# Attention block, exponentials on two engines: line 2 of most early chains added in place by a transfer, and another planned duration for VectorE's score passes

## The chip, the cores and the metric

The kernel runs on one core of a Trainium2 chip. A core has TensorE (PE; its weight loads are shown as PEld), VectorE (DVE), ScalarE (ACT), GpSimd (POOL) and SyncE (SP), each with its own in-order queue of instructions, and 16 DMA engines. The metric is the device time of one execution in microseconds, the median of several executions.

## What is computed

A multi-head attention block with its projections, for one sequence of 2048 rows, 448 columns, 16 heads of 28:

```python
B, S, D, H = 1, 2048, 448, 16
...
Dh = D // H
qkv = (lambda x, *d: x.transpose(*d))((x @ wqkv).reshape(B, S, 3, H, Dh), 2, 0, 3, 1, 4)
q, k, v = qkv[0], qkv[1], qkv[2]
scores = jnp.einsum("bhqd,bhkd->bhqk", q, k) * (Dh ** -0.5)
p = _softmax(scores, axis=-1)
o = jnp.einsum("bhqk,bhkd->bhqd", p, v)
return (lambda x, *d: x.transpose(*d))(o, 0, 2, 1, 3).reshape(B, S, D) @ wo
```

Inputs and output are bf16.

## The kernel before, in words

**Tiling.** The 16 heads form four groups `g` of four heads, each head padded to 32 partitions. The 2048 queries form four chunks `c` of 512. A pair (g, c) is a set; there are 16 sets, in the order of `ORDER`. A set has 64 score blocks: four heads times 16 blocks of 128 keys. A block is a product of 128 keys by 512 queries (line 780), made with the queries' tile `QP` and the keys' tile `KA`. Blocks of different heads use different rows of the array, and two or three run at once.

**Two engines make the exponentials.** ScalarE takes two blocks at a time from a PSUM tile `a` (two banks used in turn) and writes exponentials `pt` (line 978; ten buffers). VectorE takes single blocks from the banks `d0`, `d1` or `m` (line 993): it adds a bias and clamps at zero, as int16, and the bits read as bf16 are a piecewise linear approximation of 2 to the score's power. Four such blocks of one set, one for each head, form a chain in one tile `I` (128 x 2048, named `I4`). For a better approximation the chain is used three times: as it is (line 0), with 43 added to the bits (line 1, tile `J1`) and with 85 added (line 2, tile `J2`), each multiplied by V scaled with its own weight (`WT`; line 616 makes the scaled copies). So each VectorE block costs three products with V instead of one. All products of a set are accumulated in the bank `o` (line 1123); a column of ones in V gives the softmax's denominator.

**How lines 1 and 2 are made.** In the plain way VectorE adds the constant in one pass over the chain (line 1064). A chain that begins while at least `FAR` = 30 blocks of its set are left, in any set but the first and the last, is far: GpSimd fills `J1` with 43 (line 1029) and issues a transfer that adds `I` to it (line 1040, 512 KB), and VectorE makes line 2 only. There are four buffers of `I` and `J1`, three of `J2`.

**GpSimd** also squares K and Q for their norms (line 357) and multiplies each set's outcome by its reciprocal denominators (line 1173). `after_shared` places GpSimd's passes behind the VectorE pass that last used the port both share (`cur["shared"]`).

**What sets the order.** The kernel writes its whole instruction order by hand through a planner. `plan` simulates the engines with fixed durations (`D_EXP` 0.904 for an exponential pass, 0.6 for a score pass in `do_a`, `ACC_LAND` 5.6 from a transfer's issue to its landing, and so on), takes at each step what is ready, and emits it. Work other than the sets (projections, norms, V, output projection) stands in lists with needs, gates and priorities. `dve_ok` decides whether a block goes to VectorE: only if VectorE would be done with it before ScalarE is done with what it has. `pv_cands` sorts the products with V that are ready. Where TensorE would be idle for long, `dense` puts products with zeros. The plan is made with 24 seeds, and the one that the planner finds shortest is emitted. The engines then follow this order, held back by semaphores alone.

**V.** `VT[0]` holds V by group and block of 512 keys, groups 2 and 3 together; `VT[1]` and `VT[2]` hold the two scaled copies for all groups at once.

Of the kernel before, what the change touches and what calls it, by code (L numbers as in the profile page):

```python
# [53 lines left out]
def kernel(  # L54
# [7 lines left out]
    nc = tc.nc  # L62
# [28 lines left out]
    NPT = 10  # L91
    NCH = 4
    NCH2 = 3
    NJ = 4
    FAR = 30
    FIRST = 1
    RECLAG = 4.0
# [37 lines left out]
    WO = big.tile([P, G, D], BF16, name="WO")  # L135
    VT = [None] * NTERM
    for k in range(NTERM):
        VT[k] = {}
        for b in range(NXB):
            for g in range(GH):  # L140
                VT[k][g, b] = big.tile([P, XB, P], BF16, name=f"V{k}_{g}_{b}")[:]
        for b in range(NXB):
            t = big.tile([P, XB, G - GH, P], BF16, name=f"V{k}_{GH}_{b}")
            for g in range(GH, G):
                VT[k][g, b] = t[:, :, g - GH, :]
            VT[k][None, b] = t[:]
    xs = [big.tile([P, XB * D if b < NPL else (G - 1) * QW], BF16, name=f"xs{b}") for b in range(NXB)]
# [90 lines left out]
    def clear_v(g, b):  # L238
        v = VT[0][g, b]
        v = v.rearrange("p t g e -> p (t g e)") if g is None else v.rearrange("p t e -> p (t e)")  # L240
# [3 lines left out]
    for g in list(range(GH)) + [None]:  # L244
        for b in range(NXB):
            clear_v(g, b)
    for c in range(1, NQC):
        offs_rows(c, 0, nc.gpsimd)
    for c in range(NQC):
        offs_rows(c, 1, nc.gpsimd)  # L250

    nc.gpsimd.tensor_copy(out=identf[:], in_=ident[:])
    nc.gpsimd.memset(self_[:], 0.0)
# [4 lines left out]
    def plan(nc, tc, psum, big, wk, dram, seed, dry):  # L258
# [262 lines left out]
        def qn_first(bank, pri):  # L521
            def mm():
                held["qn0"] = (bank_tile(bank) if bank[0] != "a" else pair_tile(bank))[:, 0:QW]
                nc.tensor.matmul(out=held["qn0"], lhsT=maskK[:, 0, :], rhs=sqt.pop(("Q", 0, 0))[:], start=True, stop=True)

            def root():
                held["nq"] = VT[1][None, 0].rearrange("p t g e -> p (t g e)").bitcast(F32)
                nc.vector.tensor_scalar(out=held["nq"].bitcast(I32), in0=held.pop("qn0").bitcast(I32), scalar1=0.5,
                                        scalar2=float(127 << 22), op0=ALU.mult, op1=ALU.add)

            def scaled():
                su = held["su0"] = wk.tile([P, QW], BF16, name="su", bufs=1)
# [45 lines left out]
        def v_job(g, b, t0, bank, pri, gate=0, eng="DVE"):  # L578
# [7 lines left out]
            def mm(part):  # L586
                if part == 0:
                    held[key] = bank_tile(bank)
                for u in range(part * n // parts, (part + 1) * n // parts):
                    for cc in range(CC):  # L590
                        quarters(held[key][:, u * w:(u + 1) * w], xt(b, cc)[:, (t0 + u) * P:(t0 + u + 1) * P],
                                 WRAW[2][:, cc, g0 * HG * Dh:g1 * HG * Dh], cc == 0, cc == CC - 1)

            def evac():
                src = held.pop(key)[:, 0:n * w].rearrange("p (r e) -> p r e", e=Dh)
                if g is None:
                    dst = VT[0][None, b][:, t0:t0 + n, :, :].rearrange("p t g (i e) -> p (t g i) e", e=HP)
                else:
                    dst = VT[0][g, b].rearrange("p t (i e) -> p (t i) e", e=HP)
                if eng == "ACT":  # L600
                    nc.scalar.copy(out=dst[:, :, 0:Dh], in_=src)
                else:
                    nc.vector.tensor_copy(out=dst[:, :, 0:Dh], in_=src)

# [7 lines left out]

        def vs_job(g, b, pri):
            def scale(k):
                flat = (lambda v: v.rearrange("p t g e -> p (t g e)")) if g is None else (lambda v: v.rearrange("p t e -> p (t e)"))
                cur["shared"] = nc.vector.tensor_scalar(out=flat(VT[k][g, b]), in0=flat(VT[0][g, b]), scalar1=WT[k], scalar2=None, op0=ALU.mult)

            gs = [g] if g is not None else list(range(GH, G))
            for k in range(1, NTERM):
                add("DVE", 0.335 if g is None else 0.2, lambda k=k: scale(k), need=[("V", gs[0], XB * b + u) for u in range(XB)],  # L620
                    gives=[("VS", gg, b, k) for gg in gs], pri=pri + 0.1 * k, port=True)

# [110 lines left out]
        for b in range(NXB):  # L733
            v_job(1, b, 0, "m", 50 + b, STEPS + 10 + 12 * b)
            vs_job(1, b, 60 + b)
        a, z = 2 * STEPS, 2 * NQC * STEPS - 30
        for kt in range(0, NKT, 2):
            v_job(None, kt // XB, kt % XB, "m", 150 + kt, a + (z - a) * kt // NKT)
        for b in range(NXB):
            vs_job(None, b, 170 + b)  # L740
        for c in range(CL):
# [8 lines left out]
        pts_used = [0]  # L750
        chain = {"cur": None, "all": []}
        a_fifo = []
# [69 lines left out]
        def dve_ok(t, k):  # L822
            if chain["cur"] is None and len(chain["all"]) >= NCH:
                old = chain["all"][-NCH]
                if not j1_free() or not used_up(old, 0) or any(a[0] is old for a in adds) or old["acc"] is None or old["acc"] > t:
                    return False
            if chain["cur"] is not None and half_left(chain["cur"]["s"], 0) != half_left(chain["cur"]["s"], 1):
                return True
            fin = max(free["DVE"], t + 0.5) + 0.62 * (len(a_fifo) + k + 1) + 1.4 + 0.6 * sum(NTERM - a[2] for a in adds)
            return fin <= free["ACT"] + D_EXP * (len(exps) + max(0, left() // 2 - 2)) + 0.2 + shake(0.4)  # L830
# [29 lines left out]
        def d_more(s, t, acting):  # L860
            got, taken = [], []
            for b in d_banks(t):
# [8 lines left out]
                if ch is None:  # L871
# [3 lines left out]
                    ch[1] = wk.tile([P, HG * QW], I16, name="J1", bufs=NJ)  # L875
                    if sum(len(q) for q in remain[step[0]]) >= (FAR if step[0] < NSET - 1 else LASTFAR) and step[0] >= FIRST:
                        ch["far"] = True
# [112 lines left out]
        def do_a(t):  # L990
            r, b, pd, step, ch, n = a_fifo.pop(0)
            dst = ch["I"][:, n * QW:(n + 1) * QW]
            nc.vector.tensor_scalar(out=dst, in0=pd[:], scalar1=BIAS, scalar2=0.0, op0=ALU.add, op1=ALU.max)  # L993
            end = t + 0.6
            res[b] = end + LATS[("DVE", "PE")]
# [9 lines left out]
        def close(ch, m):  # L1005
            ch["m"] = m
            ch["at"] = free["DVE"]
            adds.append([ch, m, 2 if ch["far"] else 1])
            if ch["far"]:
                accumulate(ch, m)  # L1010

        def used_up(ch, k):
# [5 lines left out]
        def add_ok(a):  # L1018
            if a[2] == 1:
                return True  # L1020
            n = chain["all"].index(a[0])
            return n < NCH2 or used_up(chain["all"][n - NCH2], 2)

        def far_chain(ch):
# [8 lines left out]
            add("POOL", 1.05, emit, gives=[("fill", n)], pri=20, port=True)  # L1033

        def accumulate(ch, m):
            w = slice(0, m * QW)
# [5 lines left out]
            def landed(end):  # L1042
                at = ch["acc"] = end + ACC_LAND
                for n in range(m):
# [13 lines left out]
        def do_add(t):  # L1058
# [10 lines left out]
            adds[0][2] += 1  # L1069
            if adds[0][2] == NTERM:  # L1070
                adds.pop(0)
# [8 lines left out]
        def pv_cands(t):  # L1080
# [6 lines left out]
            for e in pending:  # L1087
                if e["step"][0] == s and e["ready"] <= t:
                    v = v_time(e)
                    if v is not None and v <= t:  # L1090
                        out_.append(e)
            out_.sort(key=lambda e: bool(e["ch"] and e["ch"]["far"] and e["k"] == 1 and t < e["ready"] + 1.5))
            return out_
# [14 lines left out]
        def do_pv(t, ws):  # L1108
# [9 lines left out]
            for w in ws:  # L1118
                for e in w:
                    _, i, j = e["step"]  # L1120
                    key = (s, i)
                    SETMM[key] = SETMM.get(key, 0) + 1
                    nc.tensor.matmul(out=o[HP * i:HP * (i + 1), :], lhsT=VT[e["k"]][g, j // XB][:, j % XB, HP * i:HP * (i + 1)],  # L1123
                                     rhs=e["ap"], start=(SETMM[key] == 1), stop=False, tile_position=(0, HP * i),
                                     skip_group_check=True)
                for e in w:
# [311 lines left out]
```

## Time and profile before

| What | us |
|---|---|
| Median of 3 runs (lowest to highest) | 360.37 (360.24 to 360.82) |
| The profiled execution | 360.86 |
| its span, first to last instruction | 359.1 |
| start of the first pass of line 978 | 16.9 |
| start of the last one | 349.0 |
| transfer of line 1040, issue to landing, least / median / most | 4.4 / 4.9 / 6.6 |

The clock that TensorE was granted is 0.998 over the span. The page's time by the profiler is the span; about 1.8 us of the execution lie around it. ScalarE's and TensorE's records overlap their neighbours (a pass of line 978 is recorded with 1.12 us and the next one starts 0.90 us after it), so the busy time of a group is the union of its records, and the pace is read from starts.

How the other work is spread: ten passes on ScalarE and 69 instructions on VectorE lie ahead of the first exponential pass (projections and norms of the first group, clearing of tiles); after the last one come the last set's normalisation, its output projection and the stores. In between all four engines work on the sets.

### The profile page before, as it was taken

What the parts mean: (1) busy time and instruction counts of PE and PEld (TensorE: products, weight loads), DVE (VectorE), ACT (ScalarE), POOL (GpSimd) and SP (SyncE); (2) the same over time, 40 slices, a digit from 0 to 9 for tenths busy, and PEclk for the clock granted to TensorE, in tenths of its full rate; (3) what the DMA queues carried; (4) which work ended last, traced back from release to release, by engine and by line L of the source; (5) the groups of instructions that cost most, each with busy time, mean ns of one, the idle gap of its engine ahead of it and who ended that gap; (6) DMA issues with size and microseconds to landing.
All of it is one profiled execution on the core that took longest, in us unless ns stands there. A gap on an engine that the chain in (4) does not pass through costs nothing.

```text
span 359.1 us, 11135 instructions
## 1 busy us (share of the span) xinstructions
PE 336.9 (94%) x4453; PEld 108.3 (30%) x4454; DVE 333.8 (93%) x615; ACT 339.1 (94%) x370; POOL 174.3 (49%) x215
## 2 busy tenths in 40 slices
PE   8999999999999999999989999998898989999995
PEld 4333233322234233232222222232222222222233
DVE  7889999999999999899999999998999999999973
ACT  3699999999999999999999999999999999999991
POOL 8951563635535474454455656464736464531010
PEclk9999999999999999999999999999999999999999
DMA  9430175664646666364667646565868848674111
GB/s 207 105 96 15 29 150 105 120 135 87 129 89 117 127 120 147 63 136 84 132 127 156 135 90 120 105 136 124 165 120 177 163 89 174 133 156 103 39 48 54
DMA packets 30185, 41.37 MB, mean 115 GB/s; under 512 B 15188, under 2 KB 21172, under 8 KB 30132
## 3 DMA queue, kind: packets, MB, share of 16 engines
q0 software_dynamic: 8368, 28.87, 41.6%
q1 hardware_dynamic: 20516, 11.22, 12.2%
q8 instruction: 35, 0.57, 0.6%
q10 hardware_dynamic: 1248, 0.55, 0.6%
q14 instruction: 18, 0.15, 0.1%
HBM read 6.20 MB, written 1.96 MB: 23 GB/s over the span
## 4 chain that ended last, share of the span: by engine, by line
PE 41%; ACT 32%; DVE 11%; issue 8%; DMA 6%; POOL 1%; SPq 0%; DVEq 0%; POOLq 0%; ACTq 0%
ACT pt L978 32%; PE a L780 14%; PE o L1123 11%; PE m L342 5%; DVE I L993 5%; PE m L335 4%; DMA J<-I 4%; DVE J L1064 2%; DMA rr<-scr 2%; PE o L679 1%; DMA scr<-rec 1%; PE d L780 1%; DVE KA L375 1%; DVE kp L451 1%; PE a L335 1%
## 5 line engine op out<-in xcount | busy, mean ns | idle before, releaser
L978 ACT ACTIVATE pt<-a 128x1024 bf16<-128x1024 f32 x358 | 330.5, 1121 | 3.5 <-PE a L780 1.6
L993 DVE TENSOR_SCALAR I<-d 128x512 int16<-128x512 f32 x276 | 180.3, 680 | 10.6 <-PE d L780 8.4
L780 PE MATMUL a<-QP,KA 32*128 32x512 bf16 (+1 forms) x708 | 138.1, 381 | 11.1 <-ACT pt L978 9.8
L1123 PE MATMUL o<-pt,V 128*32 128x512 bf16 x716 | 108.2, 383 | 0.0
L780 PE MATMUL d<-QP,KA 32*128 32x512 bf16 (+1 forms) x273 | 98.5, 383 | 0.2
L780 PEld LDWEIGHTS <-KA 32*128 32x128 bf16 (+1 forms) x1035 | 45.8, 91 | 145.0 <-issue 143.1
L1123 PE MATMUL o<-J,V 128*32 128x512 bf16 x616 | 87.2, 384 | 0.9 <-DVE J L1064 0.4
L1029 POOL MEMSET J<- 128x1024 int32 x55 | 58.4, 1061 | 48.4 <-PE d L780 13.5
L1040 POOL DMA_DIRECT2D J<-I x55 | 52.7, 957 | 58.1 <-DVE I L993 50.2
L1064 DVE TENSOR_SCALAR J<-I 128x2048 int16<-128x2048 int16 x99 | 73.9, 756 | 0.6
L1123 PE MATMUL o<-I,V 128*32 128x512 bf16 x308 | 68.2, 383 | 0.7 <-DVE o_sb L1150 0.6
L1123 PEld LDWEIGHTS <-V 128*32 128x32 bf16 x1640 | 31.3, 94 | 49.5 <-issue 45.3
L1173 POOL TENSOR_TENSOR xs<-o_sb,rr 128x512 bf16<-128x512 f32 x12 | 17.1, 1429 | 29.9 <-DVE J L1064 20.1
L357 POOL TENSOR_TENSOR sq<-QA 128x512 bf16<-128x512 bf16 x15 | 16.8, 1117 | 21.7 <-DVE QA L497 13.1
L993 DVE TENSOR_SCALAR I<-m 128x512 int16<-128x512 f32 x32 | 21.8, 680 | 0.2 <-PE m L780 0.2
L335 PE MATMUL m<-XT,WRAW 128*32 128x512 bf16 x216 | 18.3, 386 | 0.1
L357 POOL TENSOR_TENSOR sq<-KA 128x512 bf16<-128x512 bf16 x12 | 14.3, 1196 | 8.3 <-DVE KA L375 6.7
L342 PE MATMUL m<-WRAW,XT 128*32 128x112 bf16 (+1 forms) x432 | 13.7, 231 | 0.2
L342 PE MATMUL m<-WO,xs 128*32 128x448 bf16 x156 | 12.5, 359 | 0.0
L780 PE MATMUL m<-QP,KA 32*128 32x512 bf16 (+1 forms) x32 | 12.3, 384 | 0.0
L342 PE MATMUL m<-sq,maskK 128*32 128x512 bf16 x108 | 10.8, 389 | 1.4 <-POOL sq L357 1.2
L497 DVE CAST QA<-m 128x512 bf16<-128x512 f32 x15 | 10.2, 683 | 0.6 <-PE m L335 0.3
(126 smaller groups left out, 226.6 us busy)
## 6 DMA issues: line engine op xcount, KB each, us to landing
J<-I POOLq DMA_DIRECT2D x55, 512.0 KB, 4.9
rr<-scr SPq DMA_DIRECT2D x60, 64.0 KB
QP<-QA SPq DMA_DIRECT2D x60, 28.0 KB
out_dram<-osb SPq DMA_DIRECT2D x12, 112.0 KB
WRAW<-in_wqkv_dram SPq DMA_DIRECT2D x3, 336.0 KB
QP<-su SPq DMA_DIRECT2D x32, 2.0 KB
WO<-in_wo_dram SPq DMA_DIRECT2D x16, 24.5 KB
den<-o_sb SPq DMA_DIRECT2D x15, 8.0 KB
```

The lines of the kernel that those rows point to most:

```text
L335: nc.tensor.matmul(out=ps[HP * i:HP * (i + 1), :], lhsT=w[:, cc, h * Dh:h * Dh + HP], rhs=xt(c, cc), start=(cc == 0), stop=(cc == CC - 1), ...
L342: nc.tensor.matmul(out=out[r, :], lhsT=lhsT[:, r], rhs=rhs, start=start, stop=stop, tile_position=(0, HP * i), **k)
L357: after_shared(nc.gpsimd.tensor_tensor(out=t[:], in0=src, in1=src, op=ALU.mult))
L497: nc.vector.tensor_copy(out=t[:], in_=held[key][:, 0:QW])
L780: nc.tensor.matmul(out=out_ap, lhsT=KAt[(g, j // XB)][r, (j % XB) * P:(j % XB + 1) * P], rhs=q[r, :], start=(n == 0), stop=(n == len(terms ...
L978: nc.scalar.activation(out=pt[:], in_=ps[:], func=ACT.Exp, scale=LN2 / 128.0)
L993: nc.vector.tensor_scalar(out=dst, in0=pd[:], scalar1=BIAS, scalar2=0.0, op0=ALU.add, op1=ALU.max)
L1029: m = nc.gpsimd.memset(ch[1][:].bitcast(I32), fill)
L1040: after_shared(nc.gpsimd.dma_start(out=ch[1][:, w], in_=ch["I"][:, w], accum_op=ALU.add))
L1064: cur["shared"] = nc.vector.tensor_scalar(out=r[:, w], in0=ch["I"][:, w], scalar1=float(SHIFT[k]), scalar2=None, op0=ALU.add)
L1123: nc.tensor.matmul(out=o[HP * i:HP * (i + 1), :], lhsT=VT[e["k"]][g, j // XB][:, j % XB, HP * i:HP * (i + 1)], rhs=e["ap"], start=(SETMM[k ...
L1173: m = nc.gpsimd.tensor_tensor(out=otile(g, c), in0=st["o_sb"][:], in1=st["rr"][:], op=ALU.mult)
```

## The change

Chains come in three kinds. `own`: a chain that begins with at least `FAR2` = 44 blocks of its set left (in any set but the first and the last). VectorE makes its line 1 into `J1`. When that pass has read `I`, and TensorE has made the four products with `I` as it is, GpSimd issues a transfer that adds the constant tile `shift2` (85 in every element, filled once at the start) to `I` in place; `I` then is line 2. `far`: 30 to 43 blocks left, as before. All others: both lines by VectorE, as before.

So an own chain has no fill of `J1`, no tile `J2`, and its `I` is in use until line 2's products are done. There are six buffers of `I` and five of `J1`; room for them comes from V's scaled copies, which are now kept for two groups at a time (`VS` for groups 0 and 2, `VW` for groups 1 and 3), and made for group g once group g - 2 is finished. `VT` is one tile for group 1 and one for groups 2 and 3.

In the planner, a score pass lasts 0.615 instead of 0.6 (0.635 instead of 0.62 in `dve_ok`), a transfer's landing is counted behind the landing of the one before, at least `ACC_BUSY` = 3.0 after it (`landing`), and the products with the raw scores of an own chain go ahead of others. The last set's copy and one tile of the start (`nq`) use buffers of `pt` instead of V's.

```diff
@@ -89,10 +89,12 @@
...
     NPT = 10
-    NCH = 4
+    NCH = 6
     NCH2 = 3
-    NJ = 4
+    NJ = 5
     FAR = 30
+    FAR2 = 44
+    ACC_BUSY = 3.0
     FIRST = 1
@@ -133,17 +135,20 @@
...
     WO = big.tile([P, G, D], BF16, name="WO")
-    VT = [None] * NTERM
-    for k in range(NTERM):
-        VT[k] = {}
-        for b in range(NXB):
-            for g in range(GH):
-                VT[k][g, b] = big.tile([P, XB, P], BF16, name=f"V{k}_{g}_{b}")[:]
-        for b in range(NXB):
-            t = big.tile([P, XB, G - GH, P], BF16, name=f"V{k}_{GH}_{b}")
-            for g in range(GH, G):
-                VT[k][g, b] = t[:, :, g - GH, :]
-            VT[k][None, b] = t[:]
+    VT = {(0, b): big.tile([P, XB, P], BF16, name=f"V0_{b}") for b in range(NXB)}
+    VT[1] = big.tile([P, NKT, P], BF16, name="V1")
+    VT[2] = big.tile([P, G - GH, NKT, P], BF16, name="V2")
+    VS = {}
+    def v_of(k, g, j):
+        if k:
+            return VS[k, g, j // XB][:, j % XB, :] if g % 2 == 0 else VS[k, g][:, j, :]
+        return VT[0, j // XB][:, j % XB, :] if g == 0 else VT[1][:, j, :] if g == 1 else VT[2][:, g - GH, j, :]
+    def v_block(g, b):
+        return VT[0, b][:] if g == 0 else VT[1][:, b * XB:(b + 1) * XB, :] if g == 1 else VT[2][:, g - GH, b * XB:(b + 1) * XB, :]
     xs = [big.tile([P, XB * D if b < NPL else (G - 1) * QW], BF16, name=f"xs{b}") for b in range(NXB)]
@@ -249,6 +253,8 @@
...
+    shift2 = const.tile([P, HG * QW], I16, name="shift2")
+    nc.gpsimd.memset(shift2[:].bitcast(I32), SHIFT[2] * 65537)
     nc.gpsimd.tensor_copy(out=identf[:], in_=ident[:])
@@ -587,20 +593,23 @@
...
+                    dst = held[key][:, 0:n * w].rearrange("p (g t e) -> p g t e", g=g1 - g0, t=n)[:, :, u, :]
                     for cc in range(CC):
-                        quarters(held[key][:, u * w:(u + 1) * w], xt(b, cc)[:, (t0 + u) * P:(t0 + u + 1) * P],
-                                 WRAW[2][:, cc, g0 * HG * Dh:g1 * HG * Dh], cc == 0, cc == CC - 1)
+                        quarters(dst, xt(b, cc)[:, (t0 + u) * P:(t0 + u + 1) * P],
+                                 WRAW[2][:, cc, g0 * HG * Dh:g1 * HG * Dh].rearrange("p (g e) -> p g e", g=g1 - g0), cc == 0, cc == CC - 1)
...
@@ -611,14 +620,22 @@
...
         def vs_job(g, b, pri):
             def scale(k):
-                flat = (lambda v: v.rearrange("p t g e -> p (t g e)")) if g is None else (lambda v: v.rearrange("p t e -> p (t e)"))
-                cur["shared"] = nc.vector.tensor_scalar(out=flat(VT[k][g, b]), in0=flat(VT[0][g, b]), scalar1=WT[k], scalar2=None, op0=ALU.mult)
-            gs = [g] if g is not None else list(range(GH, G))
+                if b is None:
+                    src = VT[1][:] if g == 1 else VT[2][:, g - GH, :, :]
+                    dst = VS[k, g] = big.tile([P, NKT, P], BF16, name=f"VW{k}", tag=f"VW{k}", bufs=1)
+                else:
+                    src = v_block(g, b)
+                    dst = VS[k, g, b] = big.tile([P, XB, P], BF16, name=f"VS{k}_{b}", tag=f"VS{k}_{b}", bufs=1)
+                cur["shared"] = nc.vector.tensor_scalar(out=dst[:].rearrange("p t e -> p (t e)"), in0=src.rearrange("p t e -> p (t e)"),
+                                                        scalar1=WT[k], scalar2=None, op0=ALU.mult)
+            blocks = range(NKT) if b is None else range(XB * b, XB * (b + 1))
             for k in range(1, NTERM):
-                add("DVE", 0.335 if g is None else 0.2, lambda k=k: scale(k), need=[("V", gs[0], XB * b + u) for u in range(XB)],
-                    gives=[("VS", gg, b, k) for gg in gs], pri=pri + 0.1 * k, port=True)
+                add("DVE", 0.6 if b is None else 0.2, lambda k=k: scale(k),
+                    need=[("V", g, j) for j in blocks] + ([("Oset", ORDER.index((g - 2, CL)))] if g > 1 else []),
+                    gives=[("VS", g, j // XB, k) for j in blocks[::XB]], pri=pri + 0.1 * k, port=True)
@@ -824,9 +842,11 @@
...
                     return False
+                if old["own"] and not used_up(old, 2):
+                    return False
             if chain["cur"] is not None and half_left(chain["cur"]["s"], 0) != half_left(chain["cur"]["s"], 1):
                 return True
-            fin = max(free["DVE"], t + 0.5) + 0.62 * (len(a_fifo) + k + 1) + 1.4 + 0.6 * sum(NTERM - a[2] for a in adds)
+            fin = max(free["DVE"], t + 0.5) + 0.635 * (len(a_fifo) + k + 1) + 1.4 + 0.6 * sum(NTERM - a[2] for a in adds)
             return fin <= free["ACT"] + D_EXP * (len(exps) + max(0, left() // 2 - 2)) + 0.2 + shake(0.4)
@@ -873,7 +893,10 @@
...
                     ch[1] = wk.tile([P, HG * QW], I16, name="J1", bufs=NJ)
-                    if sum(len(q) for q in remain[step[0]]) >= (FAR if step[0] < NSET - 1 else LASTFAR) and step[0] >= FIRST:
+                    rest = sum(len(q) for q in remain[step[0]])
+                    early = FIRST <= step[0] < NSET - 1
+                    ch["own"] = early and rest >= FAR2
+                    if early and FAR <= rest < FAR2:
                         ch["far"] = True
@@ -991,7 +1014,7 @@
...
             nc.vector.tensor_scalar(out=dst, in0=pd[:], scalar1=BIAS, scalar2=0.0, op0=ALU.add, op1=ALU.max)
-            end = t + 0.6
+            end = t + 0.615
             res[b] = end + LATS[("DVE", "PE")]
@@ -1006,8 +1029,12 @@
...
             adds.append([ch, m, 2 if ch["far"] else 1])
+            if not ch["own"]:
+                chain["J2"].append(ch)
             if ch["far"]:
                 accumulate(ch, m)
+            elif ch["own"]:
+                in_place(ch, m)
@@ -1018,8 +1045,8 @@
...
                 return True
-            n = chain["all"].index(a[0])
-            return n < NCH2 or used_up(chain["all"][n - NCH2], 2)
+            n = chain["J2"].index(a[0])
+            return n < NCH2 or used_up(chain["J2"][n - NCH2], 2)
@@ -1032,6 +1059,29 @@
...
+        def landing(end):
+            chain["dma"] = max(chain["dma"], end + ACC_LAND - 1.0 - ACC_BUSY) + ACC_BUSY
+            return chain["dma"] + 1.0
+        def in_place(ch, m):
+            n = ch["id"] = chain["all"].index(ch)
+            w = slice(0, m * QW)
+            if used_up(ch, 0):
+                evt[("PV0", n)] = (free["PE"], "PE")
+            def emit():
+                after_shared(nc.gpsimd.dma_start(out=ch["I"][:, w], in_=shift2[:, w], accum_op=ALU.add))
+            def landed(end):
+                at = landing(end)
+                for q in range(m):
+                    pending.append({"step": ch["steps"][q], "k": 2, "ap": ch["I"][:, q * QW:(q + 1) * QW].bitcast(BF16),
+                                    "ready": at, "pt": None, "ch": ch})
+            add("POOL", 0.88, emit, need=[("line1", n), ("PV0", n)], gives=[("own", n)], pri=9, port=True)
+            ops["POOL"][-1].after = landed
         def accumulate(ch, m):
@@ -1040,7 +1090,7 @@
...
             def landed(end):
-                at = ch["acc"] = end + ACC_LAND
+                at = ch["acc"] = landing(end)
                 for n in range(m):
@@ -1067,7 +1117,9 @@
...
             adds[0][2] += 1
-            if adds[0][2] == NTERM:
+            if ch["own"]:
+                evt[("line1", ch["id"])] = (end, "DVE")
+            if adds[0][2] == NTERM - ch["own"]:
                 adds.pop(0)
@@ -1089,7 +1141,8 @@
...
                         out_.append(e)
-            out_.sort(key=lambda e: bool(e["ch"] and e["ch"]["far"] and e["k"] == 1 and t < e["ready"] + 1.5))
+            out_.sort(key=lambda e: 0 if not e["ch"] else -1 if e["ch"]["own"] and e["k"] == 0 else
+                      bool((e["ch"]["far"] and e["k"] == 1 or e["ch"]["own"] and e["k"] == 2) and t < e["ready"] + 1.5))
             return out_
@@ -1120,7 +1173,7 @@
...
                     SETMM[key] = SETMM.get(key, 0) + 1
-                    nc.tensor.matmul(out=o[HP * i:HP * (i + 1), :], lhsT=VT[e["k"]][g, j // XB][:, j % XB, HP * i:HP * (i + 1)],
+                    nc.tensor.matmul(out=o[HP * i:HP * (i + 1), :], lhsT=v_of(e["k"], g, j)[:, HP * i:HP * (i + 1)],
                                      rhs=e["ap"], start=(SETMM[key] == 1), stop=False, tile_position=(0, HP * i),
@@ -1131,6 +1184,8 @@
...
                         e["ch"]["got"][e["k"]] += 1
+                        if e["k"] == 0 and e["ch"]["own"] and used_up(e["ch"], 0):
+                            evt[("PV0", e["ch"]["id"])] = (end, "PE")
             if not any(remain[s]) and outst[s] == 0:
@@ -1354,7 +1409,7 @@
...
-        osb_last = [VT[1][0, hf].rearrange("p t e -> p (t e)").bitcast(F32) for hf in range(2)]
+        osb_last = [wk.tile([P, 2 * QW], BF16, name="pt", bufs=NPT)[:, 0:QW].bitcast(F32) for hf in range(2)]
         rT = [wk.tile([P, 2, HG], F32, name=f"rT{hf}", bufs=1) for hf in range(2)]
...
         work_ps = [pair_tile("a%d" % ((cur["u"] + 1) % 2))[:, 0:QW]]
@@ -524,7 +530,7 @@
...
             def root():
-                held["nq"] = VT[1][None, 0].rearrange("p t g e -> p (t g e)").bitcast(F32)
+                held["nq"] = wk.tile([P, 2 * QW], BF16, name="pt", bufs=NPT)[:].bitcast(F32)
                 nc.vector.tensor_scalar(out=held["nq"].bitcast(I32), in0=held.pop("qn0").bitcast(I32), scalar1=0.5,
```

More of the change, by code (lines that the diff above doesn't have):

```diff
@@ L238, in clear_v @@
     def clear_v(g, b):
-        v = VT[0][g, b]
-        v = v.rearrange("p t g e -> p (t g e)") if g is None else v.rearrange("p t e -> p (t e)")
+        v = v_block(g, b).rearrange("p t e -> p (t e)")
         nc.gpsimd.memset(v, 0.0)
         nc.gpsimd.memset(v.rearrange("p (r e) -> p r e", e=HP)[:, :, Dh:Dh + 1], 1.0)
-    for g in list(range(GH)) + [None]:
+    for g in range(G):
         for b in range(NXB):
@@ L589, in mm @@
                 for u in range(part * n // parts, (part + 1) * n // parts):
+                    dst = held[key][:, 0:n * w].rearrange("p (g t e) -> p g t e", g=g1 - g0, t=n)[:, :, u, :]
                     for cc in range(CC):
-                        quarters(held[key][:, u * w:(u + 1) * w], xt(b, cc)[:, (t0 + u) * P:(t0 + u + 1) * P],
-                                 WRAW[2][:, cc, g0 * HG * Dh:g1 * HG * Dh], cc == 0, cc == CC - 1)
+                        quarters(dst, xt(b, cc)[:, (t0 + u) * P:(t0 + u + 1) * P],
+                                 WRAW[2][:, cc, g0 * HG * Dh:g1 * HG * Dh].rearrange("p (g e) -> p g e", g=g1 - g0), cc == 0, cc == CC - 1)
             def evac():
-                src = held.pop(key)[:, 0:n * w].rearrange("p (r e) -> p r e", e=Dh)
+                src = held.pop(key)[:, 0:n * w]
                 if g is None:
-                    dst = VT[0][None, b][:, t0:t0 + n, :, :].rearrange("p t g (i e) -> p (t g i) e", e=HP)
-                else:
-                    dst = VT[0][g, b].rearrange("p t (i e) -> p (t i) e", e=HP)
+                    src = src.rearrange("p (g r e) -> p g r e", g=G - GH, e=Dh)
+                    dst = VT[2][:, :, b * XB + t0:b * XB + t0 + n, :].rearrange("p g t (i e) -> p g (t i) e", e=HP)[:, :, :, 0:Dh]
+                else:
+                    src = src.rearrange("p (r e) -> p r e", e=Dh)
+                    dst = v_block(g, b).rearrange("p t (i e) -> p (t i) e", e=HP)[:, :, 0:Dh]
                 if eng == "ACT":
-                    nc.scalar.copy(out=dst[:, :, 0:Dh], in_=src)
+                    nc.scalar.copy(out=dst, in_=src)
                 else:
-                    nc.vector.tensor_copy(out=dst[:, :, 0:Dh], in_=src)
+                    nc.vector.tensor_copy(out=dst, in_=src)
             for p in range(parts):
@@ L734, in plan @@
             v_job(1, b, 0, "m", 50 + b, STEPS + 10 + 12 * b)
-            vs_job(1, b, 60 + b)
+        vs_job(1, None, 60)
         a, z = 2 * STEPS, 2 * NQC * STEPS - 30
@@ L739, in plan @@
         for b in range(NXB):
-            vs_job(None, b, 170 + b)
+            vs_job(2, b, 170 + b)
+        vs_job(3, None, 180)
         for c in range(CL):
@@ L750, in plan @@
         pts_used = [0]
-        chain = {"cur": None, "all": []}
+        chain = {"cur": None, "all": [], "J2": [], "dma": 0.0}
         a_fifo = []
```

## The prediction

> **What bounds the kernel now.** I read the page's busy times first, then its groups, then busy time by stretches, then the chain of waits in order of time, and last the order in which both kernels' instructions stand on each engine.
>
> ```profile
> span 359.1 us, 11135 instructions
> PE 336.9 (94%) x4453; PEld 108.3 (30%) x4454; DVE 333.8 (93%) x615; ACT 339.1 (94%) x370; POOL 174.3 (49%) x215
> ...
> L978 ACT ACTIVATE pt<-a 128x1024 bf16<-128x1024 f32 x358 | 330.5, 1121 | 3.5 <-PE a L780 1.6
> L993 DVE TENSOR_SCALAR I<-d 128x512 int16<-128x512 f32 x276 | 180.3, 680 | 10.6 <-PE d L780 8.4
> ...
> L1029 POOL MEMSET J<- 128x1024 int32 x55 | 58.4, 1061 | 48.4 <-PE d L780 13.5
> L1040 POOL DMA_DIRECT2D J<-I x55 | 52.7, 957 | 58.1 <-DVE I L993 50.2
> L1064 DVE TENSOR_SCALAR J<-I 128x2048 int16<-128x2048 int16 x99 | 73.9, 756 | 0.6
> ```
>
> Three engines stand at 93 to 94%, so the shares don't name a limit. The stretches do: columns are length, then PE, PEld, DVE, ACT, POOL busy, clock, DMA share, GB/s.
>
> ```profile
> 16.90:100.00 83.10, 80.61 (x1283) 26.34 (x1281) 79.32 (x143) 82.12 (x89) 40.05 (x51) 1.00 0.46 96
> 100.00:200.00 100.00, 96.54 (x1268) 30.97 (x1265) 95.27 (x159) 99.85 (x110) 51.21 (x52) 1.00 0.58 118
> 200.00:300.00 100.00, 91.78 (x1040) 26.89 (x1036) 96.39 (x161) 98.35 (x108) 55.04 (x55) 1.00 0.65 131
> 300.00:350.20 50.20, 48.56 (x603) 14.84 (x601) 46.80 (x81) 50.20 (x55) 12.72 (x12) 1.00 0.45 102
> ```
>
> ScalarE is busy 330.5 of these 333.3 us, VectorE 317.8. ScalarE's exponentials overlap in the record, so I price one by the distance between starts. The chain shows that distance where nothing disturbs it, 0.90 us:
>
> ```profile
> 161.21 0.72 ACT pt L978
> ...
> 162.12 0.69 ACT pt L978
> ...
> 163.02 0.75 ACT pt L978
> ```
>
> The first of 358 exponentials starts at 16.9, the last at 349.0 (the line's own view), so 357 distances take 332.1 us. At 0.904 (the median over the trace) they would take 322.7. So the span is 16.9 ahead, 322.7 of ScalarE at its pace, 9.4 us lost, and 10.1 from the last start to the end. Only the 9.4 can be won while the number of exponentials stays.
>
> **Where the 9.4 us go.** Going through the records, 15 of the 99 VectorE passes at L1064 took over 720 ns. The 99 together are 99 x (756 - 683, the median) = 7.2 us too long. One of them, from the timeline of VectorE and of GpSimd:
>
> ```profile
> 198.41 1.54 DVE L1064 TENSOR_SCALAR J<-I 128x2048 int16<-128x2048 int16 x1
> ```
> ```profile
> 198.14 1.26 POOL L1029 MEMSET J<- 128x1024 int32 x1
> ```
>
> The pass ends about 0.55 us after GpSimd's fill: it stood still beside it. Five long passes lie beside such a fill (121.0, 190.0, 198.4, 211.9, 252.2; 3.1 us above the median together), seven beside a square at L357, two beside a product at L1173, one beside a transfer's issue. The exponentials that start within 5 us after a long pass come 4.05 us late in sum, 1.54 of it after the five fills. A second loss is a transfer that lands late:
>
> ```profile
> 178.82 6.50 DMA J<-I
> ...
> 237.26 6.60 DMA J<-I
> ```
>
> Both stand on the chain; exponentials after them come 0.33 and 0.68 us late, 1.0 together. The start costs 0.6 (distances at 19 to 22 us). The remaining 3.8 us is scattered: a group's key statistics at 152.9, products at 87 and 222, single steps.
>
> **The change part by part.** The order of instructions of the changed kernel shows the same 358 exponentials and 308 score passes on VectorE, so the change does take effect without moving work between the two engines. Nothing new stands before the first exponential but the fills of V.
>
> *Second lines in place.* 38 chains no longer have GpSimd's fill and copy-accumulate of line 1; VectorE makes line 1, and a GpSimd-issued transfer adds a constant to the chain's own scores. 16 chains keep the old form. GpSimd loses 39 x 1.061 = 41.4 us of fills; transfers go from 55 to 54 of 512 KB, so DMA traffic stays (the software queue's 41.6% of 359.1 over 55 is 2.7 us each). VectorE's passes go from 99 to 100 (+0.68), its V scalings from 16 x 0.348 + 8 x 0.498 to 16 x 0.348 + 4 x 0.683 (-1.25): nothing. The gain is in collisions: 39/55 of the fills' 1.54 us, -1.1 (bounds: -1.54, and 0 if the new order only puts squares in their place).
>
> The Trainium skill, page "SBUF — State Buffer", section "SBUF: two separate sides", says that VectorE in its fast modes and GpSimd take one port pair as a lock, and the later waits for the whole of the other. The trace agrees (1.54 beside 0.68 us). The same section adds that GpSimd can't write the descriptors of its transfers while VectorE holds that lock. That speaks against the change, since the 54 issues stay; here 11 of 55 issues took 1.17 to 1.42 us instead of 0.87.
>
> *The planner's duration, 0.60 to 0.615 us.* Back to back, a score pass takes 0.60 (two in 1.28, the second starting 0.60 after the first). So each of 308 passes gets 0.015 us more than it needs, 4.6 us of VectorE in all, with which it catches up after being late. I give it 1.5 us of what is left: 9.4 - 1.1 - 1.0 - 0.6 is 6.7, of which VectorE's remaining lateness after long passes (4.05 - 1.1 = 2.95) is the part it can reach, and half of that is 1.5. Bounds: 0, and -4.6.
>
> *Transfers counted one after another.* The planner now lets a transfer occupy the queue 3.0 us, more than the 2.7 above, and puts uses of a line back accordingly. The two late landings stood 3.1 and 3.0 us behind the transfer ahead. I take -0.7 of their 1.0 (bounds -1.0 and 0).
>
> *The new wait.* The in-place issue waits for VectorE's line 1 and for TensorE's products with the chain's raw scores. Behind it in GpSimd's order stand fills, squares and products, and the next transfer; TensorE waits for squares (1.2 us in all now), the output projection for products. GpSimd is idle 51%, which covers it. What isn't covered is a late landing: TensorE takes its instructions in order, so it would hold the next scores. In the order, 8 to 17 score steps lie between the last raw product and the first product with line 2, 7.2 to 15.4 us at 0.904; the 55 landings took 4.4 to 6.6 from issue. The chains' buffers also come free only then: in ten places 0 to 3 steps lie between a buffer's last read and its next write, where before the least was 3. I take +0.5 (bounds 0 and +5.4, eight waits like that at 244.7).
>
> *The rest at nothing.* Clearing V goes from 10.8 us to 16 x (0.543 + 0.169) = 11.4, and the constant's fill adds 1.06; behind them on GpSimd stand 14 small transfers and then a square that waits 4.56 us for VectorE, which covers it, or 1.7 if not. The 44 further matmuls with zeros (11 groups of four) are set where TensorE has a gap. V's products and evacuations have other strides and as many elements. Two small tiles moved into ScalarE's output ring delay one exponential, 0.9, if their slot is late; at the end no exponential is left.
>
> Sum: -1.1 - 1.5 - 0.7 + 0.5 = -2.8. The profiled execution took 360.86, of which 359.1 is span; it becomes 358.1. The median of the runs shown is 0.49 lower, 360.37, so I predict **357.6**.
>
> **Rivals.** *Landings become the wait (slower).* Eleven times two in-place transfers are issued for the same or the next score step, which never happened before (the closest issues were 2.7 us apart). A second transfer then lands about 2.7 us after the first, 7.1 to 9.3 us after its issue, with 11 to 15 steps (9.9 to 13.6) to spare, and a third or fourth of the same set behind it. It decides where issue and landing together pass 7.2 us for a first transfer. Seven chains have 8 or 9 steps; at 0.68 each that is 4.8, and with the gain by collisions and half of the slack kept (-1.9) and -0.7 gone, the time is 360.4 + 4.8 - 1.9 = 363.3. For it: long issues, landings up to 6.6. Against: the median landing is 4.9, and the planner's 3.0 is above the 2.7. The skill's page "DMA: Bandwidth & Descriptors", section "Anatomy of one DMA — SWDGE (gpsimd) path", has 2.0 us plus bytes over 436 GB/s, 3.2 for this size as an estimate; the trace's 4.4 to 6.6 decides here.
>
> *No change.* The new order puts as many passes beside squares and products as beside fills, and slack is used up waiting for TensorE, for which VectorE now waits 8.4 us in L993's group. Time 360.4, within 0.2%, that is 0.7 us, about the least that a measurement of this kernel can tell.
>
> *Slack absorbs all lateness of VectorE.* Then the whole 2.95, the scattered 3.8 in half, the fills' 1.1 and the landings' 1.0 go, nothing comes: 2.95 + 1.9 + 1.1 + 1.0 = 7.0, 353.4. For it: 4.6 us of spare time plus VectorE's 15.5 us idle in the stretches above. Against: stalls of TensorE by key statistics don't end with it.
>
> **Chances.** Forecast (355.0 to 359.6) 0.44, all absorbed 0.13, no change 0.15, landings 0.28. Faster 0.57, same 0.15, slower 0.28. The range goes from 353.8, most of the absorbed case, to 363.0, most of the landings case; the forecast's own range is 355.0 to 359.6.
>
> **What would show it.** L978 still x358 and L993's two groups 308 together. GpSimd's fills at x16 and its busy time near 174.3 - 41.4 + 1.7 = 135. The mean of the L1064 passes falls from 756 towards 735. VectorE's idle time before L993 grows. The distance between first and last exponential falls from 332.1 to about 329. In the waits, TensorE's time behind transfers stays under 2 us. I am wrong if TensorE waits for in-place transfers by several us, if L993 waits for a buffer, or if long passes at L1064 stay at 15 beside squares and products.

## The result, and the profile after

| | before | changed |
|---|---|---|
| Median of 4 runs (lowest to highest) | 360.60 (360.24 to 361.25) | 370.69 (369.93 to 370.90) |
| Span of the profiled execution | 359.1 | 369.1 |
| First and last start of ScalarE's 358 passes | 16.9, 349.0 | 17.0, 358.6 |
| Lost between them (357 distances of 0.904 = 322.7) | 9.4 | 18.9 |

Medians, here and below, leave out the few executions that were slow.

The changed kernel takes 1.0271 of the time before (95% interval 1.0252 to 1.0290), where I had forecast 357.6. The start and the end stay as they were (10.5 us from the last start to the end, 10.1 before); the loss lies between ScalarE's passes. The page of the changed kernel:

```profile
span 369.1 us, 11114 instructions
PE 344.5 (93%) x4498; PEld 109.3 (30%) x4498; DVE 328.7 (89%) x612; ACT 339.8 (92%) x370; POOL 134.4 (36%) x184
...
L1001 ACT ACTIVATE pt<-a 128x1024 bf16<-128x1024 f32 x358 | 331.2, 1147 | 12.3 <-PE a L798 7.9
L1016 DVE TENSOR_SCALAR I<-d 128x512 int16<-128x512 f32 x279 | 182.7, 681 | 24.1 <-PE d L798 14.7
...
L1114 DVE TENSOR_SCALAR J<-I 128x2048 int16<-128x2048 int16 x100 | 70.0, 712 | 0.9
...
L1056 POOL MEMSET J<- 128x1024 int32 x16 | 20.0, 1296 | 0.6 <-DVE J L1114 0.6
...
I<-shift POOLq DMA_DIRECT2D x38, 512.0 KB, 5.6
J<-I POOLq DMA_DIRECT2D x16, 512.0 KB, 8.0
```

Much of the forecast is there: 358 passes, GpSimd at 134.4 us (135 forecast), 16 fills, and VectorE's pass over a chain shorter, 712 ns in the mean instead of 756. But ScalarE is idle 12.3 us ahead of its passes instead of 3.5, and VectorE 24.1 instead of 10.6 ahead of L1016. The waits of the changed kernel (engine and line, what it waited for, us in total, times, longest) name who is behind that:

```profile
DVE I L1016 <- DMA J<-I: 8.1, 4, 3.4
ACT pt L1001 <- PE a L798: 7.9, 7, 3.6
...
PE d L798 <- DVE I L1016: 5.7, 5, 2.6
...
PE o L1176 <- DMA I<-shift: 0.2, 1, 0.2
```

In four places VectorE waits for a transfer before it writes scores into I; TensorE waits for VectorE to free a bank; ScalarE waits for TensorE. The last row is TensorE's whole wait for in-place transfers, 0.2 us. One of these places in the timelines of VectorE, TensorE and ScalarE (start, length, instruction, idle time ahead of it):

```profile
184.18 0.79 DVE L1114 TENSOR_SCALAR J<-I 128x2048 int16<-128x2048 int16 x1
188.36 0.69 DVE L1016 TENSOR_SCALAR I<-d 128x512 int16<-128x512 f32 x1 [3.40 <-DMA J<-I]
```
```profile
189.10 0.58 PE L798 MATMUL d<-QP,KA 32*128 32x512 bf16 x1 [2.62 <-DVE I L1016]
```
```profile
191.30 1.02 ACT L1001 ACTIVATE pt<-a 128x1024 bf16<-128x1024 f32 x1 [3.59 <-PE a L798]
```

The chain of waits has the transfer itself, as a piece 9.45 us long:

```profile
178.81 9.45 DMA J<-I
```

It is a far chain's copy: it reads I and adds it to J1. So VectorE doesn't wait for an in-place transfer. It waits to overwrite an I that a far chain's copy is still reading. In the built program's addresses that far chain is only the third before the one that VectorE begins (the third in three of the four places, the fourth in one). The planner supposes the sixth: `dve_ok` lets a chain begin when `chain["all"][-NCH]` is done with, NCH being 6. The addresses show how far back the chain is whose buffer each new chain gets: before, the fourth in all 73 cases (NCH 4). In the changed kernel the third in 4 cases, the fourth in 12, the fifth in 11, the sixth in 16, the seventh to ninth in 28. In nearly all cases (68 of 71) the pool gives out the buffer whose last use was emitted first, and an own chain's I is used until its line 2 is done with; a far chain's is released earlier, and passes it.

ScalarE's passes just after these four waits (they end at 188.4, 275.3, 290.3 and 316.0) and after the two of VectorE for TensorE that follow from them (193.9 and 325.2) come 11.9 us late in sum. Apart from them ScalarE loses 7.0, less than the 9.4 before.

### The profile page after: what moved, and what is told of

It is laid out like the page before. It is cut to its first block, busy times and chain, and to the rows that moved or that the text cites. A ratio compares the mean times of both kernels' runs of the same rounds, so it can differ in the third digit from the quotient of the medians.

```text
span 369.1 us, 11114 instructions
## 1 busy us (share of the span) xinstructions
PE 344.5 (93%) x4498; PEld 109.3 (30%) x4498; DVE 328.7 (89%) x612; ACT 339.8 (92%) x370; POOL 134.4 (36%) x184
## 4 chain that ended last, share of the span: by engine, by line
PE 57%; ACT 18%; DMA 12%; DVE 5%; issue 4%; SPq 2%; POOL 1%; DVEq 0%; POOLq 0%; ACTq 0%
PE a L798 21%; ACT pt L1001 18%; PE o L1176 18%; DMA J<-I 8%; PE m L348 7%; PE m L341 6%; DVE I L1016 3%; DMA scr<-rec 2%; DMA XT<-in_x_dram 1%; PE d L798 1%; DVE J L1114 1%; SPq L176 1%; DVE kp L457 1%; SPq L187 1%; DMA rr<-scr 1%
## 5 line engine op out<-in xcount | busy, mean ns | idle before, releaser
L1001 ACT ACTIVATE pt<-a 128x1024 bf16<-128x1024 f32 x358 | 331.2, 1147 | 12.3 <-PE a L798 7.9
L1016 DVE TENSOR_SCALAR I<-d 128x512 int16<-128x512 f32 x279 | 182.7, 681 | 24.1 <-PE d L798 14.7
L1176 PE MATMUL o<-pt,V 128*32 128x512 bf16 x716 | 98.6, 385 | 0.0
L1114 DVE TENSOR_SCALAR J<-I 128x2048 int16<-128x2048 int16 x100 | 70.0, 712 | 0.9
L1176 PE MATMUL o<-I,V 128*32 128x512 bf16 x308 | 60.2, 391 | 0.7 <-DVE o_sb L1205 0.7
L1074 POOL DMA_DIRECT2D I<-shift x38 | 33.8, 939 | 64.3 <-PE o L1176 37.6
L1176 PE MATMUL o<-J,VW 128*32 128x512 bf16 x248 | 37.7, 391 | 0.4 <-DVE J L1114 0.4
L1176 PEld LDWEIGHTS <-V 128*32 128x32 bf16 x1024 | 25.2, 95 | 29.5 <-issue 28.1
L1176 PE MATMUL o<-J,VS 128*32 128x512 bf16 x216 | 32.1, 387 | 0.0
L1016 DVE TENSOR_SCALAR I<-m 128x512 int16<-128x512 f32 x29 | 19.7, 679 | 0.6 <-DMA J<-I 0.6
L1056 POOL MEMSET J<- 128x1024 int32 x16 | 20.0, 1296 | 0.6 <-DVE J L1114 0.6
L1090 POOL DMA_DIRECT2D J<-I x16 | 17.5, 1091 | 7.3 <-DVE I L1016 4.2
L1176 PEld LDWEIGHTS <-VW 128*32 128x32 bf16 x328 | 10.9, 95 | 17.3 <-issue 16.5
```

Source lines behind the costliest of these rows:

```text
L1001: nc.scalar.activation(out=pt[:], in_=ps[:], func=ACT.Exp, scale=LN2 / 128.0)
L1056: m = nc.gpsimd.memset(ch[1][:].bitcast(I32), fill)
L1074: after_shared(nc.gpsimd.dma_start(out=ch["I"][:, w], in_=shift2[:, w], accum_op=ALU.add))
L1090: after_shared(nc.gpsimd.dma_start(out=ch[1][:, w], in_=ch["I"][:, w], accum_op=ALU.add))
L1114: cur["shared"] = nc.vector.tensor_scalar(out=r[:, w], in0=ch["I"][:, w], scalar1=float(SHIFT[k]), scalar2=None, op0=ALU.add)
L1176: nc.tensor.matmul(out=o[HP * i:HP * (i + 1), :], lhsT=v_of(e["k"], g, j)[:, HP * i:HP * (i + 1)], rhs=e["ap"], start=(SETMM[key] == 1), s ...
```

## The experiments

"Rotating" below means one edit: six names for the buffers of I with one buffer each, so that each chain gets the sixth before it.

**The same plan with rotating buffers, and three more.**

```diff
-                    ch = chain["cur"] = {"I": wk.tile([P, HG * QW], I16, name="I4", bufs=NCH), "s": step[0], "n": 0,
+                    ch = chain["cur"] = {"I": wk.tile([P, HG * QW], I16, name="I4", tag=f"I4_{len(chain['all']) % NCH}", bufs=1), "s": step[0], "n": 0,
```

> The changed kernel with the same plan, but each chain takes the buffer of I that the sixth chain before it had (six names with one buffer each), which is what the planner assumes; the pool by itself gives out the buffer released first, often that of a far chain three or four chains back whose transfer still reads it. Theory BUFFER (VectorE waits for such a buffer, ScalarE after it; 11.9 us of late exponentials follow the five longest such waits): 370.7 - 11.9 = 358.8, between 357.5 and 360, and the waits of the score pass for J<-I gone. Theory LANDING (bursts of transfers land late and the products wait for them wherever the buffers are): 369 to 371. Theory DURATION (the planner's 0.615 spoils the order): unchanged, 370 to 371.

Measured: 363.14 (362.15 to 363.60), 1.0056 of the time before (1.0035 to 1.0077). All five engines have the same instructions in the same order as in the changed kernel. The addresses of I are the whole difference, and they are worth 370.69 - 363.14 = 7.5 us. No wait of L1016 for J<-I is left, and the distances between buffers are 6 in all 71 cases. Theory BUFFER holds in the place; in size it is 4.3 us short, because another wait is large here that was small (0.5 us) in the changed kernel:

```profile
PE m L348 <- POOL OTL L1228: 3.1, 2, 1.9
```

TensorE's output projection waits for GpSimd's product with the reciprocal denominators. Late exponentials after its two places (293 to 299 and 339) are 4.8 us. SyncE's queue shows why, first in the rotating kernel, then at the same point of the kernel before:

```profile
281.76 0.33 SPq L1219 DMA_DIRECT2D scr<-rec  x1
290.09 1.96 SPq L1225 DMA_DIRECT2D rr<-scr  x4
```
```profile
281.71 0.33 SPq L1164 DMA_DIRECT2D scr<-rec  x1
285.02 2.15 SPq L1170 DMA_DIRECT2D rr<-scr  x4
```

The 8 KB transfer of the reciprocals to memory takes 8.3 us until the next may start, 3.3 before. In the rotating kernel five transfers of 512 KB are issued from 275.0 to 280.9. The DMA packets in the trace show the small transfer waiting among them: its 128 packets of 64 bytes run from 4.9 to 7.7 us after its issue, where in the kernel before they run from 1.8 to 2.8.

The planner's durations of before in the rotating kernel:

```diff
-            end = t + 0.615
+            end = t + 0.6
...
-            fin = max(free["DVE"], t + 0.5) + 0.635 * (len(a_fifo) + k + 1) + 1.4 + 0.6 * sum(NTERM - a[2] for a in adds)
+            fin = max(free["DVE"], t + 0.5) + 0.62 * (len(a_fifo) + k + 1) + 1.4 + 0.6 * sum(NTERM - a[2] for a in adds)
```

> As the run with rotating buffers, with the planner's durations of before (0.6, and 0.62 in the choice of blocks). The plan then gives ScalarE 356 exponentials and VectorE 312 passes instead of 358 and 308. If the longer duration buys the 1.5 us of slack that the prediction gave it, this is 1.5 - 2 x 0.904 = about 0.3 us faster than the rotating one, that is the same; if the longer duration buys nothing, it is 1.8 us faster; if VectorE without slack is late more often, 1 to 3 us slower. Theory DURATION: about 359, and the rotating one stays at 370.

Measured: 357.38 (356.62 to 359.53), 0.9917 of before (0.9885 to 0.9950). It is 5.8 us faster than the rotating kernel with 0.615, none of my cases. No wait for a product with reciprocals is left in it. Whether the duration or chance of the plan did that, the second group tells.

The new durations alone in the kernel before (the same two lines the other way round):

> The kernel before with the planner's 0.615 and 0.635 alone. The plan moves four blocks to ScalarE: 360 exponentials and 304 passes, +1.8 us at 0.904 each. If the slack is worth the 1.5 us of the prediction: 360.7, the same within 0.7. If it is worth nothing: 362.2. Theory DURATION: 366 or more. Theories BUFFER and LANDING say nothing of it.

Measured: 361.19 against 360.94, ratio 1.0008 (0.9998 to 1.0019). In its profile ScalarE's 359 distances have a mean of 0.926 us, 8.0 us above 0.904 each; before they are 9.4. So in this plan ScalarE loses 1.4 less, near the 1.5 of the prediction, and the two further exponentials cost 1.8. One plan against one plan can't tell whether the 1.4 is the longer duration's or chance.

The changed kernel without own chains:

```diff
-    FAR2 = 44
+    FAR2 = 99
```

> The changed kernel with no own chains (the bound of 44 blocks set to 99): all early chains are far as before, with six buffers of I, five of J1, V's new layout and the new planned durations. 53 transfers of the old kind, 360 exponentials. Theory BUFFER: all early chains release alike, so no such waits; within 1 us of the kernel before with the new durations alone, 360 to 362.5. Theory LANDING: the same, as transfers are spread again. If the new layout of V or the counting of landings costs anything by itself, it is slower than that by as much.

Measured: 360.97, ratio 1.0011 (0.9988 to 1.0034). So V's new layout, six buffers and the new count of landings show no cost by themselves; the interval allows -0.4 to 1.2 us. ScalarE loses 6.5 us in this profile, less than the 9.4 before, without any own chain.

**What is left of the rotating kernel: transfers behind bursts, or chance.** The second group changes the planner's landing of the small transfer, and takes other plans.

```diff
-            add("SP", 0.35, scatter, need=[("rec", s)], gives=[("scr", s)], land=1.1, pri=2)
+            add("SP", 0.35, scatter, need=[("rec", s)], gives=[("scr", s)], land=7.0, pri=2)
```

> The rotating kernel (363.1), with one more number of the planner changed: the 8 KB transfer of a set's reciprocals to memory counts 7.0 us to its landing instead of 1.1. In the rotating run it took 6 to 9 us in sets 10 to 14, behind bursts of four 512 KB transfers, where it took 2.7 to 4.6 in the kernel before, and TensorE waited 3.1 us for the products with the reciprocals. Theory BURST (small transfers stand behind the bursts; what the planner sets too early on them costs the rest): 363.1 less the 4.8 us of late exponentials after those waits, 358 to 359.5. Theory PLAN (the rest is chance of the plan): anywhere between 357 and 366, with the wait for the product of another size but still there.

Measured: 361.47 (360.35 to 362.27), ratio 1.0017 (1.0001 to 1.0033). The wait for the product is gone, and ScalarE's loss falls from 11.5 to 6.8 us, by the 4.7 expected. But only 1.7 of it reaches the median. In the profiled executions the gain is 2.8 (363.18 to 360.35; the second is the fastest of its ten): more output projection is put off, and the stretch after ScalarE's last pass is 10.9 us with 108 matmuls, where the rotating kernel has 9.4 with 102 and the kernel before 8.9 with 84. So neither theory's forecast holds in full: BURST is right about the wait and not about the time, and PLAN, whose range holds, expected the wait to stay. Its row of busy time by stretches (length, PE, PEld, DVE, ACT, POOL, clock, DMA share, GB/s):

```profile
347.60:358.50 10.90, 6.39 (x108) 3.69 (x105) 3.26 (x8) 1.52 (x4) 0.59 (x1) 0.95 0.17 54
```

> The rotating kernel with the durations of before (357.4) and the 7.0 us as well. The plan has 358 exponentials and 308 passes, two exponentials more than without the 7.0. Theory BURST: there was no wait for a product left in that run, so +1.8 for the exponentials and no gain: 358.5 to 360. Theory PLAN: between 357 and 364.

Measured: 361.12, ratio 1.0005 (0.9991 to 1.0020), slower than without the 7.0 by 3.7, of which two exponentials are 1.8.

```diff
-    seed = min(ends, key=lambda k: ends[k])
+    seed = sorted(ends, key=lambda k: ends[k])[1]
```

> The rotating kernel with the plan that the planner ranks second among its seeds, everything else equal (358 exponentials, 308 passes). It shows how much of the 5.8 us between the two rotating kernels is chance of the plan. Theory PLAN: off 363.1 by 2 us or more. Theory BURST: the same waits for the products, 361 to 365. Theory DURATION (0.615 costs 4 us by itself): 362 to 364.

Measured: 360.02 (359.07 to 361.90), ratio 0.9982 (0.9962 to 1.0002).

> The rotating kernel with the durations of before and the plan ranked second (358 exponentials, 308 passes). Theory DURATION: 357 to 360, as the first seed with 0.6 plus 1.8 for two exponentials. Theory PLAN: off 359.2 by 2 us or more on either side.

Measured: 362.65 (360.20 to 363.42), ratio 1.0037 (1.0011 to 1.0063), with 3.6 us of waits for the product with reciprocals. With 0.615 the two seeds gave 363.1 and 360.0, with 0.6 they gave 357.4 and 362.7: the duration has no effect that stands out from chance of the plan. Theory DURATION falls, theory PLAN fits best, and BURST names one thing that chance decides: whether the output projection is put ahead of the late product.

**The buffers once more, in another plan, and the fastest version again.** The changed kernel with the durations of before and the pool's own choice, then the fastest of the first group a second time:

> The changed kernel with the planner's durations of before, and the pool's own choice of buffers: the same instructions in the same order as the rotating kernel with these durations (357.4), only the addresses of I differ. 15 chains take the buffer of the third or fourth chain before them (16 in the changed kernel). Theory BUFFER: 5 to 10 us slower than the rotating one, 362 to 368, with VectorE waiting for J<-I and TensorE for VectorE behind it. Theory DURATION: as fast as the rotating one, 357 to 359, since the 0.615 is gone.

Measured: 367.64 (366.01 to 369.12), ratio 1.0179 (1.0145 to 1.0213), the same instructions in the same order as the rotating kernel of 357.4. Again in the waits:

```profile
DVE I L1016 <- DMA J<-I: 9.0, 3, 4.3
```

> The rotating kernel with the durations of before once more, beside the same plan without rotation: 356.5 to 358.5, faster than the kernel before by 0.4 to 1.2%. If the 357.4 was chance of a chip, 359 or more.

Measured: 358.26 (357.48 to 359.67), ratio 0.9926 (0.9906 to 0.9946). So in this plan the pool's choice costs 9.4 us, and the rotating version beats the kernel before by 0.7% and the changed kernel by some 12 us.

## Why the prediction was wrong

**What failed: the new wait, taken at +0.5.** I wrote that "in ten places 0 to 3 steps lie between a buffer's last read and its next write". For that I paired each chain with the sixth before it, as the planner does, and counted TensorE's reads only. The addresses would have shown that 16 chains get the buffer of the third or fourth before them, in 13 cases that of a far chain; and in the four places where VectorE waits, the last reader of that I is a transfer, not TensorE. The wait measured +7.5 us in the changed kernel's plan and 9.4 in a second one, outside my upper bound of 5.4 too. One of my signs of being wrong, "if L993 waits for a buffer", came true (the line is L1016 in the changed kernel). I had the right resource (the buffers "come free only then") and the wrong owner.

**The rival for the slower side had the wrong place.** Landings did get later, with a median of 8.0 us and a most of 10.3 for the far copies, mostly issued last in a burst; the rival had a second landing at 7.1 to 9.3. But TensorE, which I let wait for them, waited 0.2 us in all for in-place transfers. The likely reason is the planner's 3.0 us for each, which puts the uses later; no run is without it. What wasn't moved back was VectorE's next write, and, in the rotating plan, the small transfer of the reciprocals. The rival's price, seven waits of 0.68, has no measurement behind it now.

**Transfers counted one after another, -0.7.** The part on products holds: they hardly wait. What I left out is that the same bursts delay other transfers; the planner counts that of the reciprocals apart, at 1.1 us, and it took 6 to 9 us in sets 10 to 14 of the rotating kernel. So "GpSimd is idle 51%, which covers it" failed for the output projection: GpSimd had the time, but its product waits for the reciprocals, and TensorE for the product, 3.1 us.

**Collisions, -1.1.** As forecast, long passes became fewer: ten passes at L1114 took over 720 ns instead of 15, two of them beside a fill instead of five. But that this comes from the fills is not shown. The kernel before with the new durations alone has seven long passes with 53 fills, and the rotating kernel's second seed has 12 with 15 fills, so the count goes with the plan too. What it brought to ScalarE was not measured apart.

**The slack, -1.5.** The run of the new durations in the kernel before loses 1.4 less, but in one plan, and the two seeds above show no effect of the duration. I had read from equal counts of exponentials that it costs nothing; alone, it costs two exponentials, 1.8 us.

**Edits at nothing.** Layout of V, more buffers and zeros: the run without own chains shows the time of before within its interval, as taken.

**Sum.** In the rotating kernel ScalarE loses 11.5 us, 4.8 after waits for products; the other 6.7 is 2.7 less than the 9.4, near the 3.3 that the three gains make. That is no proof of them, since the run without own chains loses as little, 6.5. Over the six rotating plans (357.4, 360.0, 361.1, 361.5, 362.7 and 363.1) the mean is 361.0, the time of before. One of the six reaches the forecast -2.8, and as plans of nearly the same kernel lie this far apart, I count that one as luck; a gain of 2.8 us that comes with the change in any plan isn't seen. How far the plans of the kernel before lie apart was not measured. I gave no term to the plan at all.

## What to carry to other kernels

Where a planner reasons about buffers by age, look up in the built program which buffer each tile really got: as soon as lifetimes differ, a pool that gives out the first released one passes the old ones over, and a still reading transfer becomes the wait. A transfer that reads a buffer is a reader like any engine. When large transfers are bunched, ask also what small transfer stands behind them, and judge a re-planned order by several plans, since here plans of nearly the same kernel differ by up to 5.8 us.

## What the runs showed of the hardware

TensorE's clock fell after these stalls, which I hadn't reckoned with. The rows are busy time by stretches in the changed kernel (length, busy time of PE, PEld, DVE, ACT and POOL, clock, DMA share, GB/s):

```profile
184.90:188.30 3.40, 1.56 (x21) 0.51 (x18) 0.07 (x1) 2.81 (x4) 0.00 (x0) 1.00 0.56 111
...
189.00:194.00 5.00, 4.90 (x29) 0.83 (x32) 3.37 (x8) 2.15 (x3) 0.00 (x0) 0.50 0.16 32
...
314.60:318.00 3.40, 1.68 (x17) 0.30 (x14) 2.04 (x4) 1.76 (x2) 0.00 (x0) 1.00 0.13 33
```

The granted clock is 0.50 in the second of these stretches, and matmuls that took 0.39 us are recorded with 0.58 to 0.63. The clock record has 0.5 from 188.3 for 6.8 us and from 318.0 for 6.8 us, and 1.0 otherwise from 4.0 to the end. The first fall comes 1.8 us into TensorE's idle time of 2.62 us, the second 1.3 us after the end of one of 1.72; in the 3.4 us ahead of each, TensorE was busy for 1.56 and 1.68 us. Of the 11.9 us, 2.6 lie in exponentials that start in these two stretches after the first one in each; how much of that is the clock alone was not measured apart. The Trainium skill, page "TensorE: Matmul & The Clock Gate", section "Part 1: The HAM clock gate (the "warmup" mystery)", has the clock at half after an idle window of about 3.4 us, until activity releases it; the trace agrees on the half, and its stretches are twice that window. It differs on the idle window: here the clock fell though TensorE was busy for nearly half of the 3.4 us ahead.

A 512 KB transfer from GpSimd's queue landed 4.4 us after its issue at the least and 4.9 in the median in the kernel before, whose issues are 2.7 us or more apart. In the changed kernel's bursts of three to five within 6 us the last took up to 10.3. An 8 KB transfer from SyncE's queue took 6 to 9 us until the next one in sets 10 to 14 of the rotating kernel, and 2.7 to 4.6 in the same sets of the kernel before.
